# Searched per-batch orders, a rewritten first batch and a new load order in an attention-plus-MLP kernel

## The chip, the cores and the metric

One core of a Trainium2 chip. The metric is the device time of one launch in microseconds (us), which includes about 2 us outside the span of the profile. A run over 1.5% above the fastest of its kernel counts as slow. "PE" is TensorE, "DVE" VectorE, "ACT" ScalarE, "POOL" GpSimd.

## The reference

Eight batches of Nystrom attention (8 heads, 576 tokens, head size 64, 32 landmarks), then one MLP with squared ReLU over all 4608 tokens.

```python
q_lm, k_lm = segment means of q, k over 18 tokens each          # 32 landmarks
A  = softmax(q @ k_lm.T / 8);  Bm = softmax(q_lm @ k_lm.T / 8);  C = softmax(q_lm @ k.T / 8)
Z  = Bm.T / (norm1(Bm) * norminf(Bm) + 1e-6)
for _ in range(6): Z = 2*Z - Z @ Bm @ Z                          # iterative inverse
x   = A @ Z @ C @ v                                              # per head, then heads side by side
out = relu(x @ w_in)**2 @ w_out                                  # w_in 512x2048, w_out 2048x512
```

## The kernel before

It never forms x. For each batch it makes G = (Z C v) w_in, of which each half is 128 x 2048, and AT, the transposed A. A hidden block of 128 features, called h, is four matmuls of 288 columns from AT and G; then relu on ACT, the square on DVE, and 16 matmuls with w_out for each output tile. The six iterations of the inverse are three joint steps, a last joint step and two Newton steps, each with its products on PE and its update on DVE. In the steady state PE runs the h blocks of batch b, output tiles of earlier batches, and the small attention products of batch b+1 in between. The places of all of these are written as strings, which are followed token by token. PE, DVE and ACT work through their queues in that order.

```python
# tokens: h = one h block, s = its square, a number = so many output matmuls,
# mk mq = segment means, tk tq tt = transposes, lm ls = landmark scores and softmax, ib if = start of
# the inverse, jo jl = joint steps, nu nn = B times v and Newton step, sq sk tl = scores with exp,
# as ar at = A's row sums, rows, transposes, cv = C v, wt gg = fold and G, pk pq = cast of next k, q
BATCH0 = (
    "h h s s g h pk s h s h h g s h s h s tk0 h h s pq mk s h s h mq tq0 h s s 2 lm ls s h "
    "tk1 ib tq1 1 h h 1 tt 1 if 2 s 1 sq0 1 jo s 2 sq1 jo s 1 tl jo 2 as0 3 sk1 jl 3 ar0 3 "
    "sk0 2 as1 1 nu at0 2 ar1 nn pk+ 1 cv 1 nu nn1 1 at1 wt pq+ 2 gg0 2 gg1"
)
...                                                   # BATCH1, EVEN, ODD, LAST
PLANS = [BATCH0, BATCH1, EVEN, ODD, EVEN, ODD, EVEN, LAST]
```

The first batch has nothing beside which it could run. Its order is code, and PE's gaps are partly filled with warm-up matmuls, whose results nobody reads, to keep PE's clock up.

```python
def warm(n, width=512):
    z = bds[1].rearrange("p a b c -> p (a b c)")
    for _ in range(n):
        nc.tensor.matmul(idle[:, 0:width], lhsT=z[:, 0:P], rhs=z[:, 0:width], start=True, stop=True)
...
if first:
    prepare(0, ("k",))                # cast k: half on DVE, half on ACT
    load_rest(X["cast"])              # w_in(0), v0, w_in(1..3), q/k of batch 1, w_out x4, v1
    warm(3)
    k0 = transposed("k", 0)
    k1 = transposed("k", 1)
    kept = dve(*k0)
    ...                               # q's cast, means, landmark scores and softmax
    BT, ED = inverse_first(*begun)
    ...
for it in range(3):
    EY, ED, last = joint_step(EY, ED)
    ...                               # each step with a piece of A's or C's work aside
y, v = last_joint_step(EY, ED)
for it in range(2):
    UD = b_times_v(BT, v)
    y, v, last = newton_step(y, UD, it == 1)
    ...
wt, WT = folded_c(y.rearrange("p q a m -> p q (a m)"))
nc.scalar.copy(WT[:], wt[:])
warm(2)
...                                   # G from WT and w_in, copied by ACT and DVE; then h
```

The softmax here doesn't subtract the row's maximum and nothing guards it: scores larger than these inputs give would overflow.

## Time and profile before

| before | value | where it is read |
|---|---|---|
| time | 269.76 us (269.14 to 270.24) | three runs |
| span | 267.4 us | page |
| PE busy | 93% | page, part 1 |
| DVE, ACT busy | 66%, 59% | page, part 1 |
| first h block | 25.0 us | timeline of PE |
| first h block of batch 1 | 54.8 us | timeline of PE |

From the page of the kernel before: each digit is the busy share, in tenths, of one of 40 slices of 6.7 us, PEclk is the clock granted to PE.

```profile
PE   2988999699989999999999999999999999999994
DVE  4585989769983699559953798569943887443000
PEclk9997999999999999999999999999999999999999
```

PE is full but for the first 27 us and one slice near 50 us. The busy time by stretches (columns: stretch, its length, busy us and number of instructions of PE, PE's weight loads, DVE, ACT and POOL, then granted clock, DMA share, GB/s) says more:

```profile
20.00:25.00 5.00, 3.72 (x56) 1.79 (x53) 2.88 (x9) 2.41 (x7) 1.55 (x3) 0.70 1.40 197
25.00:37.00 12.00, 11.56 (x153) 8.58 (x147) 10.19 (x25) 10.79 (x23) 4.59 (x7) 0.98 1.32 204
37.00:54.00 17.00, 13.81 (x195) 7.72 (x196) 14.69 (x43) 9.26 (x15) 6.82 (x9) 1.00 1.53 198
```

In 20-25 us the granted clock is 0.70 on average: it is cut to half for part of the time. In 37-54 us PE is idle for 3.2 of 17 us. The timeline of PE (start, busy us, line, operation, count, and in brackets the idle time before and what ended it) has the landmarks of the head:

```profile
1.52 1.46 PE L234 MATMUL idle<-bd 128*128 128x512 bf16 x3 [1.52 <-DVE bd L90]
6.89 1.89 PE L258 MATMUL tps<-ident_bf,nat 128*128 128x128 bf16 x16 [3.90 <-POOL mask L142]
...
12.10 0.25 PE L315 MATMUL n<-STk,bd 128*128 128x32 bf16 x4
...
21.17 0.22 PE L357 MATMUL n<-y,U 32*32 32x32 bf16 x8 [0.39 <-ACT cvb L525]
...
24.99 1.33 PE L700 MATMUL h<-AT,G 128*128 128x288 bf16 x8
...
49.77 0.21 PE L357 MATMUL n<-y,ED 128*128 128x32 bf16 x2 [1.67 <-DVE ED L348]
```

The 16 transposes of k begin at 6.89 us, the landmark scores at 12.10, the last product of the inverse at 21.17, the first h at 24.99. One Newton step of batch 1 at 49.77 has made PE wait 1.67 us for DVE.

The pace of the first joint steps is in the timeline of DVE (L362 is the update, L464 a row sum of A):

```profile
15.81 0.29 DVE L362 SCALAR_TENSOR_TENSOR EY<-EY,n 128x128 bf16<-128x128 bf16 x1 [0.35 <-PE n L357]
16.01 0.41 DVE L464 TENSOR_REDUCE ra<-EA 128x8 f32<-128x256 f32 x1
16.45 0.29 DVE L362 SCALAR_TENSOR_TENSOR EY<-EY,n 128x128 bf16<-128x128 bf16 x1
```

### The profile page before, as it was taken

To read this page: it belongs to the slowest core of one execution; us is meant where nothing else is said; L and a number is where in the kernel's file an instruction comes from. 1 tells how busy PE (TensorE), PEld (TensorE's weight loads), DVE (VectorE), ACT (ScalarE), POOL (GpSimd) and SP (SyncE) were. 2 spreads that over 40 slices of the span, in tenths; PEclk is the share of its full clock that TensorE was granted. 3 is DMA by queue.
4 is the path that set the end of the run, shared out by engine and by line. 5 is a ranking of instruction groups with operands and counts; after the bars stand their busy time and mean duration, and the time that the engine had idled before them with its cause. 6 is when DMAs were issued, how large, how long until landed. Compare 5 with 4: busy or idle time off the path is not lost.

```text
span 267.4 us, 6750 instructions
## 1 busy us (share of the span) xinstructions
PE 247.7 (93%) x2752; PEld 151.0 (56%) x2793; DVE 177.4 (66%) x492; ACT 156.9 (59%) x278; POOL 45.5 (17%) x70
## 2 busy tenths in 40 slices
PE   2988999699989999999999999999999999999994
PEld 0754675276645665466546666466536665555443
DVE  4585989769983699559953798569943887443000
ACT  2366895377844774478345855487535955566210
POOL 8844233402400213021300122000000000000000
PEclk9997999999999999999999999999999999999999
DMA  8999999999699949995996579974421111111222
GB/s 184 177 204 196 204 205 189 206 210 165 103 161 214 126 95 158 142 206 99 201 159 132 78 94 171 168 134 110 90 81 40 42 39 42 39 43 39 78 81 78
DMA packets 69791, 34.65 MB, mean 130 GB/s; under 512 B 37376, under 2 KB 64256, under 8 KB 69760
## 3 DMA queue, kind: packets, MB, share of 16 engines
q0 software_dynamic: 39808, 17.83, 54.9%
q1 hardware_dynamic: 24704, 7.08, 17.7%
q10 hardware_dynamic: 5248, 9.31, 10.5%
q8 instruction: 22, 0.36, 0.6%
q14 instruction: 9, 0.07, 0.1%
HBM read 36.70 MB, written 9.44 MB: 173 GB/s over the span
## 4 chain that ended last, share of the span: by engine, by line
PE 60%; DVE 22%; DMA 6%; ACT 6%; issue 4%; POOL 2%; ACTq 0%; POOLq 0%; DVEq 0%
PE ops L732 18%; PE n L732 15%; PE h L700 14%; DMA raw<-in_q_dram 6%; DVE gT L708 5%; PE g L639 3%; DVE ra L464 3%; ACT r L707 3%; PE n L285 2%; DVE nat L220 2%; PE n L357 2%; PE n L486 2%; DVE ED L348 1%; DVE EY L362 1%; DVE rra L469 1%
## 5 line engine op out<-in xcount | busy, mean ns | idle before, releaser
L707 ACT ACTIVATE r<-h 128x576 bf16<-128x576 f32 x128 | 81.3, 655 | 40.6 <-PE h L700 30.1
L700 PE MATMUL h<-AT,G 128*128 128x288 bf16 x512 | 81.0, 286 | 0.7 <-ACT r L707 0.4
L732 PE MATMUL ops<-w_out_bf,gT 128*128 128x512 bf16 (+1 forms) x301 | 76.7, 368 | 1.0 <-issue 0.5
L708 DVE TENSOR_TENSOR gT<-r 128x576 bf16<-128x576 bf16 x128 | 55.5, 446 | 31.5 <-ACT r L707 30.7
L732 PEld LDWEIGHTS <-gT 128*128 128x128 bf16 x592 | 53.4, 97 | 40.6 <-issue 5.1
L732 PE MATMUL n<-w_out_bf,gT 128*128 128x512 bf16 x253 | 67.6, 379 | 0.9 <-issue 0.5
L700 PEld LDWEIGHTS <-G 128*128 128x128 bf16 x512 | 47.5, 98 | 22.3 <-issue 1.5
L628 DVE CAST G<-g 128x1024 bf16<-128x1024 f32 x14 | 17.1, 1224 | 10.5 <-PE g L639 10.5
L628 ACT CAST G<-g 128x1024 bf16<-128x1024 f32 x14 | 14.2, 1013 | 14.7 <-PE g L639 14.7
L743 ACT COPY o_sb<-ops 128x512 f32<-128x512 f32 (+1 forms) x19 | 10.9, 576 | 12.3 <-PE ops L732 11.9
L743 ACT COPY o_sb<-n 128x512 f32<-128x512 f32 x17 | 10.0, 585 | 10.9 <-PE n L732 10.3
L109 POOL DMA_DIRECT2D qkt<-in_k_dram x8 | 5.7, 708 | 54.3 <-PE n L295 42.7
L440 PEld LDWEIGHTS <-T 128*128 128x128 bf16 x256 | 11.2, 98 | 4.3 <-issue 1.0
L464 DVE TENSOR_REDUCE ra<-EA 128x20 f32<-128x640 f32 (+1 forms) x19 | 13.4, 705 | 0.3
L476 DVE TENSOR_TENSOR an<-EA,rra 128x640 bf16<-128x640 f32 (+2 forms) x17 | 13.1, 771 | 0.0
L440 PE MATMUL n<-bd,T 128*128 128x64 bf16 x256 | 12.7, 193 | 0.2
L357 PEld LDWEIGHTS <-ED 128*128 128x128 bf16 x84 | 7.1, 97 | 9.3 <-DVE ED L348 5.9
L121 POOL DMA_DIRECT2D raw<-in_k_dram x7 | 6.2, 884 | 32.4 <-DVE EY L362 12.4
L444 ACT ACTIVATE EA<-n 128x512 f32<-128x512 f32 x16 | 9.5, 595 | 2.3 <-PE n L440 2.3
L444 ACT ACTIVATE EC<-n 128x512 bf16<-128x512 f32 x16 | 9.6, 598 | 2.1 <-PE n L440 2.1
L220 DVE COPY nat<-raw 128x2048 bf16<-128x2048 bf16 x14 | 10.3, 734 | 0.6 <-DMA raw<-in_q_dram 0.4
L639 PE MATMUL g<-w_in_bf,WT 64*32 64x512 bf16 x232 | 9.6, 390 | 0.7 <-ACT G L628 0.4
(121 smaller groups left out, 268.1 us busy)
## 6 DMA issues: line engine op xcount, KB each, us to landing
out_dram<-o_sb ACTq DMA_DIRECT2D x31, 256.0 KB, 3.2
vm<-in_v_dram POOLq DMA_DIRECT2D x8, 512.0 KB, 16.4
raw<-in_k_dram POOLq DMA_DIRECT2D x7, 512.0 KB, 9.9
raw<-in_q_dram POOLq DMA_DIRECT2D x7, 512.0 KB, 13.8
w_in_bf<-in_moe_w_in_dram POOLq DMA_DIRECT2D x4, 512.0 KB, 10.7
w_out_bf<-in_moe_w_out_dram POOLq DMA_DIRECT2D x4, 512.0 KB, 16.1
out_dram<-o_sb ACTq DMA_DIRECT2D x9, 128.0 KB, 3.2
raw<-in_k_dram SPq DMA_DIRECT2D x1, 1024.0 KB, 5.3
```

The lines of the kernel that those rows point to most:

```text
L220: nc.vector.tensor_copy(X[nm][:], raw)
L440: nc.tensor.matmul(sc[:, c, j, :, :], lhsT=X[nm + "T"][:, c, p, :], rhs=BD[:, 1 if nm == "q" else 0, p, 0:64], start=True, stop=True)
L444: nc.scalar.activation((EA if nm == "q" else EC)[:, qd, 0:NC4, :], sc.rearrange("p c j i m -> p c (j i m)"), AF.Exp, scale=SCALE)
L464: nc.vector.reduce_sum(ra[:, quads, lo:hi, :], EA[:, quads, lo:hi, :].rearrange("p q c (h m) -> p q c h m", m=M), axis=AX.X)
L476: nc.vector.tensor_tensor(an[:, i, lo:hi, :].rearrange("p c (h m) -> p c h m", m=M), EA[:, i, lo:hi, :].rearrange("p c (h m) -> p c h m", ...
L628: last = (act, dve)[n % 2](G[:, :, n * 512:n * 512 + 512], gg[:])
L639: nc.tensor.matmul(g[i][M * p:M * p + M, :], lhsT=WT[64 * i:64 * i + 64, i, M * p:M * p + M], rhs=w_in_bf[64 * i:64 * i + 64, p, n * 512:n ...
L700: last = nc.tensor.matmul(h[:, j, 0:HALF], lhsT=G[:, qd, f * P:(f + 1) * P], rhs=AT[:, qd, j * HALF:(j + 1) * HALF], start=(qd == 0), stop ...
L707: nc.scalar.activation(r.rearrange("p (j t) -> p j t", j=2), h[:, :, 0:HALF], AF.Relu)
L708: return lambda: nc.vector.tensor_tensor(gT[:, f, o:o + S], r[:], r[:], ALU.mult)
L732: nc.tensor.matmul(ops, lhsT=gT[:, f, t * P:t * P + P], rhs=w_out_bf[:, f, i * n:i * n + n], start=(f == 0), stop=(f == NF - 1))
L743: nc.scalar.copy(o_h, ops)
```

## The change

Its intent: the orders of all eight batches come from a search (annealing) that rewards an early first h and few warm-up matmuls. The first batch becomes an order (HEAD) too. It takes four joint steps, the last one, and one B-times-v pair in place of three, one and two. G is made from C v alone while the inverse still runs, and Z is multiplied onto A instead ("az"). q and k of batches 0 to 2 are loaded to a staging area, and half of w_in goes behind q and k of batch 1. Batch 1 uses the compact inverse, with 32 x 32 tiles, that only batch 0 had. The two halves of k's and q's transposes have a PSUM tile each. The diff, cut to its core:

```diff
-PLANS = [BATCH0, BATCH1, EVEN, ODD, EVEN, ODD, EVEN, LAST]
+DMA_A = 9
+DMA_C = 9
+COMPACT = 1
+HEAD = (
+    "ck tk1 mk w:1:256 w:1:256 ek1d w:1:256 w:1 tk0 tt w:1 w:1 cq0 cq1 ek0a mq tq0 tq1 lm "
+    "w:1 et w:1:256 w:1 eq0a w:1:256 tl eq1d ls sum:0:4:5 w:1 ib w:1 w:1:256 sq1 w:1:256 if "
+    "sk1 sum:1:2:5 w:1:256 w:1 sum:1:0:2 jo w:1:256 w:1:256 rec:1 w:1:256 row:1:0:3 "
...
+    "jl at:0 ea0d ea1a ct w:1:256 nu w:1:256 g:0 gl1d fv w:1 gf1d w:1 gf0a az gl0d"
 )
+LOADS = "w10 v0 w00 q1 w01 w11 o0 o1 o2 o3 v1"
+PLANS = [
+    (
+        "pk h g:1 tt h pq h s tk1 s h s h tq1 s tk0 h h mk s s mq tq0 h lm s g:2 g:3 ls sk0 s h "
+        "h ib 1 h 1 s if tl h jo 1 sq0 s 1 jo s s 1 h jo 1 sq1 1 jl h 1 nu h s s h nn 2 sk1 nu s "
+        "1 s 8 as0 1 ar0 as1 2 ar1 5 nn1 cv 4 wt at0 2 gg0 2 at1 2 gg1 1"
+    ),
...                                                   # seven more
@@ load_rest
+        with tc.issue_after(behind[0].ins):
+            nc.gpsimd.tensor_copy(seg[:, NC4 + 2, :], seg[:, NC4, :])
+            for i in range(2):
+                ct = const.tile([P, 2, NC4 + 1, P], BF16, name="ct%d" % i)
+                nc.gpsimd.memset(ct[:], 0.0)
+                cts.append(ct)
@@ head_step
+            elif name == "az":
...
+                            nc.tensor.matmul(az[j][a:a + M, qd, 0:HALF],
+                                             lhsT=st["v"][a:a + M, qd, :],
+                                             rhs=AT[a:a + M, qd, j * HALF:j * HALF + HALF],
+                                             start=True, stop=True)
```

In HEAD, w:1 is one warm-up matmul 512 columns wide and w:1:256 one of 256; ck and cq cast k and q, ek and eq copy the transposes out, sum, rec and row are pieces of A's softmax, and a and d at the end of a token say ACT or DVE. The buffers ct belong to a variant for batches from DMA_C on; with DMA_C = 9 nothing reads them. HEAD has 35 warm-ups where there were 14.

## The prediction

> **What bounds it now.** TensorE. The page gives PE 247.7 us busy of 267.4 (93%), DVE 66%, ACT 59%. PE's 19.7 idle us are uneven. By windows, PE is busy 16.8 of the first 25 us, 13.8 of 17 us in 37-54, and 9.6 to 9.95 of every 10 us from 80 to 250. The timeline puts the first h matmul at 25.0 us, batch 1's first h at 54.8, and an even-odd pair of batches at 58.7 us. After the last matmul (263.8) come 3.6 us of copy and store. The h and output matmuls (128 groups of 0.49 us; 576 at 0.216) are about 187 us and stay.
>
> **What changes.**
>
> 1. Head. Before: three joint steps (0.63 us each), a last one, two Newton pairs (about 1.7 us each), then spread 0.29, fold matmul, copy 0.37, G matmul 0.63, G copy 0.37, with the transposed A landing late (ACT copy ending 25.2). Now: four joint steps, a last one, one pair; G is made from the C side meanwhile, and Z is multiplied onto A in small tiles. After the last DVE step (21.66 before) there remain one group of AZ matmuls and two 288-column copies, about 1.2 to 1.5 us, against 3.3. A joint step for a Newton pair is worth about 1 us more. DVE evacuations ahead of the landmark softmax give back a few tenths. First h: 21.7 us (20.8 to 23.2).
>
> 2. Clock. The granted clock is 0.70 in 20-25 and 0.98 in 25-37: about 3.4 us at half rate, after PE pauses at 20.4-22.7. The Trainium skill ("TensorE: Matmul & The Clock Gate", Part 1) gives one activity window as 3413 ns; this trace agrees. Warm-up matmuls rise from 14 to 35. I expect no half-clock stretch around the first h; its gain is inside item 1.
>
> 3. Batches 0 and 1. Before, batch 0's 16 h go in 25-38, paced by ACT (relu 0.65 us against 0.49 of matmul), then 37-54 has only 35 output matmuls to hide batch 1's inverse: 3.2 us idle, 1.8 of them one Newton step waiting for DVE. Now h is spread over the plan, batch 1 uses the compact inverse (no 0.29 us spreads), and 38 outputs fit: 4.5 us. First h of batch 1: about 47.5 us.
>
> 4. Loads. Same bytes, same 1024-column pieces; w_in's second half goes behind batch 1's q and k; q/k of batches 1 and 2 go to staging without a buffer wait. The DMA runs at about 200 GB/s through the first 50 us; batch 2's q lands at 51.75 before, by my estimate from bytes at 49.5 to 51 after. Its cast may hold DVE for 1 to 2 us, which caps item 3.
>
> 5. Steady state, 60-250: perhaps 2.5 us from reordering, mostly in 60-80. Tail unchanged.
>
> Sum: 3.3 + 4.5 + 2.5 = 10.3, less 0.8 for mis-modelled stalls: 9.5 us.
>
> **Prediction: 260.3 us, range 256.5 to 265.** Chances: faster by over 2% 0.88, within 2% 0.10, slower 0.02.
>
> **What would show it.** First h near 21.7; granted clock 1.00 in 20-30; PE idle in 37-54 about 1 us; batch 1's first h near 47.5, with DVE waiting for raw q near 50; pair period 58 us; 3.6 us after the last matmul.
>
> **What would make it wrong.** The head bound by the landing of q or w_in rather than the chain; warm-up matmuls standing ahead of chain steps on PE's ordered queue; DVE blocked at batch 1's early casts (k lands about 23 us by my estimate) so that squares and h buffers stall; the gain given back waiting for batch 2's loads; the searched orders losing over 2 us in the steady batches.

## The result

The changed kernel takes 265.97 us (265.86 to 266.55, 4 runs) against 269.47 (269.14 to 270.24, 4 runs). Ratios are computed as the mean time of one kernel's fast runs over that of the other's of the same rounds, so they are not quite the ratio of the medians quoted. The ratio is 0.987, with an interval of 0.984 to 0.990: 1.3% faster, which is within the 2% to which the prediction gave a chance of 0.10. Predicted was 260.3, in a range of 256.5 to 265. The measured time lies above the range.

The page after:

```profile
PE   0799899999999999999999999999999999999994
DVE  3488986879985779689766589689776884232100
PEclk9999999999999999999999999999999999999999
```

The stretches that answer to those of before:

```profile
20.00:25.00 5.00, 4.78 (x134) 3.07 (x134) 4.06 (x14) 1.86 (x5) 3.12 (x4) 1.00 1.46 201
25.00:37.00 12.00, 10.54 (x157) 7.16 (x146) 11.21 (x21) 10.05 (x19) 5.70 (x8) 1.00 1.20 208
37.00:54.00 17.00, 16.46 (x243) 9.43 (x245) 12.74 (x37) 9.98 (x20) 5.35 (x7) 1.00 1.51 200
```

The half clock in 20-25 is gone and 37-54 has only 0.5 us of idle PE, as predicted. But 25-37 has become worse, with 1.5 us idle. And the head is not earlier, by the timeline of PE:

```profile
8.01 1.03 PE L315 MATMUL tps<-ident_bf,nat 128*128 128x128 bf16 x8 [8.01 <-ACT nat L720]
...
9.41 1.23 PE L297 MATMUL idle<-bd 128*128 128x256 bf16 x4
10.44 1.06 PE L315 MATMUL tps<-ident_bf,nat 128*128 128x128 bf16 x8
...
11.72 1.06 PE L297 MATMUL idle<-bd 128*128 128x512 bf16 x2
...
14.29 0.26 PE L374 MATMUL n<-STk,bd 128*128 128x32 bf16 x4
...
23.77 0.22 PE L416 MATMUL n<-U,y 32*32 32x32 bf16 x8
...
25.68 0.65 PE L824 MATMUL h<-AZ,G 128*128 128x288 bf16 x4 [0.41 <-DVE AZ L797]
```

Nothing runs on PE before 8.01 us; the 8 transposes start 107 ns apart again; the landmark scores begin at 14.29 us, 2.2 us later than before, and the first h at 25.68, 0.7 later. The spans by step, each the difference of two starts in these two traces:

| step, us | before | after | gain |
|---|---|---|---|
| start to k's cast (its load has landed) | 6.13 | 6.91 | -0.78 |
| k's cast to landmark scores | 5.97 | 7.38 | -1.41 |
| landmark scores to end of the last iteration step on DVE | 9.56 | 10.26 | -0.70 |
| from there to the first h | 3.33 | 1.13 | +2.20 |
| first h to first h of batch 1 | 29.82 | 29.99 | -0.17 |
| first h of batch 1 to the end | 212.60 | 209.16 | +3.44 |
| span | 267.41 | 264.84 | +2.57 |

The orders issue 41 output matmuls before the first h of batch 1 instead of 37, so 0.86 us (4 x 0.216) of the gain in the last stretch was paid for in the stretch before it. The traces were taken of one run each; the timed medians differ by 3.5 us, and the row of k's landing is within the scatter (over the runs below it came at 6.3 to 7.0 us in the changed kernel and its variants, and at 6.79 in c1, a variant of the kernel before).

The joint steps stand further apart on DVE (L421 is the update now; reciprocals and rows of A come between two of them):

```profile
18.28 0.28 DVE L421 SCALAR_TENSOR_TENSOR EY<-EY,n 128x128 bf16<-128x128 bf16 x1
18.48 0.27 DVE L579 RECIPROCAL rra<-ra 128x20 f32<-128x20 f32 x1
18.78 0.89 DVE L586 TENSOR_TENSOR an<-EA,rra 128x384 bf16<-128x384 f32 x2
19.59 0.28 DVE L421 SCALAR_TENSOR_TENSOR EY<-EY,n 128x128 bf16<-128x128 bf16 x1
```

One more line stands out, in the timeline of DVE of the changed kernel, beside that of POOL below it:

```profile
26.21 0.68 DVE L283 COPY nat<-stage 128x2048 bf16<-128x2048 bf16 x1
...
27.80 2.54 DVE L283 COPY nat<-stage 128x2048 bf16<-128x2048 bf16 x1
```

```profile
27.36 0.22 POOL L261 COPY seg<-seg 128x32 bf16<-128x32 bf16 x1
27.50 2.28 POOL L264 MEMSET ct<- 128x1280 bf16 x2
```

The same cast of 128 x 2048 took 0.68 us at 26.21 and 2.54 at 27.80, while POOL cleared the ct buffers from 27.50 to 29.78. The cast ends 0.55 us after the clearing does. The Trainium skill ("SBUF — State Buffer", Who interferes with whom) says that GpSimd and a DVE instruction in a 2-port perf mode, which a copy from SBUF to SBUF can enter, exclude each other for a whole instruction. Here the cast was held through both clearing instructions. That made the first theory.

### The profile page after: what moved, and what is told of

Its sections match the earlier page's. It is cut to its first block, busy times and chain, and to the rows that moved or that the text cites. A ratio compares the mean times of both kernels' runs of the same rounds, so it can differ in the third digit from the quotient of the medians.

```text
span 264.8 us, 6918 instructions
## 1 busy us (share of the span) xinstructions
PE 248.2 (94%) x2835; PEld 153.7 (58%) x2878; DVE 176.4 (67%) x485; ACT 158.5 (60%) x278; POOL 47.8 (18%) x73
## 4 chain that ended last, share of the span: by engine, by line
PE 87%; DVE 5%; DMA 2%; issue 2%; ACT 2%; ACTq 0%
PE ops L853 24%; PE h L824 22%; PE n L853 21%; PE n L532 3%; PE g L807 3%; DMA stage<-in_k_dram 2%; PE idle L297 2%; PE n L416 2%; PE n L344 2%; PE n L598 2%; PE n L616 1%; DVE nat L283 1%; DVE gT L829 1%; PE tps L315 1%; PE n L631 1%
## 5 line engine op out<-in xcount | busy, mean ns | idle before, releaser
L829 DVE TENSOR_TENSOR gT<-r 128x576 bf16<-128x576 bf16 x128 | 54.9, 448 | 26.3 <-ACT r L828 26.1
L824 PE MATMUL h<-AT,G 128*128 128x288 bf16 x448 | 71.0, 286 | 0.2
L853 PE MATMUL n<-w_out_bf,gT 128*128 128x512 bf16 x252 | 69.7, 379 | 1.1 <-issue 0.3
L864 ACT COPY o_sb<-ops 128x512 f32<-128x512 f32 (+1 forms) x19 | 10.9, 574 | 14.5 <-PE ops L853 14.5
L134 POOL DMA_DIRECT2D raw<-in_k_dram x5 | 4.6, 921 | 53.2 <-DVE gT L829 28.1
L574 DVE TENSOR_REDUCE ra<-EA 128x20 f32<-128x640 f32 (+3 forms) x19 | 13.2, 704 | 0.3 <-ACT EA L562 0.3
L532 PE MATMUL n<-bd,T 128*128 128x64 bf16 x256 | 12.7, 193 | 0.3 <-issue 0.2
L315 PEld LDWEIGHTS <-nat 128*128 128x128 bf16 x96 | 6.8, 108 | 9.8 <-ACT nat L720 8.0
L134 POOL DMA_DIRECT2D raw<-in_q_dram x5 | 4.4, 884 | 38.5 <-DVE rc L447 28.1
L315 PE MATMUL tps<-ident_bf,nat 128*128 128x128 bf16 x32 | 3.4, 278 | 8.0 <-ACT nat L720 8.0
L824 PE MATMUL h<-AZ,G 128*128 128x288 bf16 x64 | 10.0, 286 | 0.6 <-DVE AZ L797 0.4
```

The lines of the kernel that those rows point to most:

```text
L134: d = queue.dma_start(dst, src)
L315: nc.tensor.transpose(tps[:, i, p, :], X[nm][:, 2 * half + i, 2 * p:2 * p + 2, :].rearrange("p h d -> p (h d)"), ident_bf[:],)
L532: nc.tensor.matmul(sc[:, c, j, :, :], lhsT=X[nm + "T"][:, c, p, :], rhs=BD[:, 1 if nm == "q" else 0, p, 0:64], start=True, stop=True)
L574: nc.vector.reduce_sum(ra[:, quads, lo:hi, :], EA[:, quads, lo:hi, :].rearrange("p q c (h m) -> p q c h m", m=M), axis=AX.X)
L824: nc.tensor.matmul(h[:, j, 0:HALF], lhsT=G[:, qd, f * P:(f + 1) * P], rhs=AT[:, qd, a0 + j * HALF:a0 + (j + 1) * HALF], start=(qd == 0), s ...
L829: return lambda: nc.vector.tensor_tensor(gT[:, f, o:o + S], r[:], r[:], ALU.mult)
```

## The experiments

Fifteen kernels ran; all gave the right result. To compare heads, the table at the end of this section counts from k's cast, to take the chance of its landing out. Runs told together below ran on the same chip beside the same runs of before.

### First call: the head's start and the clearing

The theories: (a) PE is the chain of the head's start, because it is at half clock there and has six warm-ups ahead of q's means in its ordered queue; (b) the clearing of ct blocks DVE. The rival to both is that waiting for data sets these times.

**a0_same**: no edit.

> The changed kernel again, as the base of this call. All theories: 266.0 us, ratio to before 0.987, first h matmul at 25.3 to 25.8 us. If raw k lands near 6.1 us here instead of 6.9, the late landing in the first profile was chance and the first h comes about 0.6 us earlier.

Measured: 265.71 us, ratio 0.984; k's cast at 6.32, first h at 24.23. Landing and the clock's phase move the head by over a microsecond from run to run; the times of the six runs go from 264.5 to 266.4.

**a1_no_ct**

```diff
-                nc.gpsimd.memset(ct[:], 0.0)
```

> The two memsets of the ct buffers on GpSimd, which nothing reads, are taken out. Port theory (the DVE cast of batch 1's q stood 2.54 us instead of 0.68[...]): the cast takes 0.7 us, h matmuls of batch 0 come 1.5 to 1.9 us earlier after it, total 264.3 to 265.0 us. Rival (the cast was waiting for its data to land, the memsets are harmless): the cast starts later or stays long, total 266.0 us, same as the base.

Measured: 265.12 us, ratio 0.982. The timeline of DVE:

```profile
25.55 0.68 DVE L282 COPY nat<-stage 128x2048 bf16<-128x2048 bf16 x1
...
27.14 0.68 DVE L282 COPY nat<-stage 128x2048 bf16<-128x2048 bf16 x1
```

Both casts take 0.68 us, and the first h to batch 1's first h takes 29.00 us instead of 30.12. In the time it is worth 0.6 us by the medians, less than was expected and within the scatter of the base; in the trace the effect is plain.

**a2_early_warm**

```diff
-    "ck tk1 mk w:1:256 ...
+    "ck w:14 tk1 mk w:1:256 ...
```

> 14 warm-up matmuls at the very start, in time in which PE otherwise waits for k (0 to 8 us). Clock theory (the head is late because all PE work from 8.0 to 13.7 us runs at half clock and PE is the chain there): transposes of k issue every 56 ns instead of 104, the q means come 1.2 to 2 us earlier, first h near 24.0 us, total 264.2 to 265.0. Rival (the head is bound by q's landing and by the chain on DVE and ACT, not by PE): q means move by less than 0.5 us and the total stays within 0.4 us of the base.

Measured: 264.12 us, ratio 0.978. The timeline of PE:

```profile
1.53 5.67 PE L297 MATMUL idle<-bd 128*128 128x512 bf16 x14 [1.53 <-DVE bd L117]
7.82 0.62 PE L315 MATMUL tps<-ident_bf,nat 128*128 128x128 bf16 x8 [0.63 <-ACT nat L720]
...
12.08 0.26 PE L374 MATMUL n<-STk,bd 128*128 128x32 bf16 x4
```

The transposes issue every 56 ns; the trace's clock record has full speed from 6.6 us on. From k's cast to the landmark scores it is 5.36 us instead of 6.53: theory (a). In this run the clearing happened to miss the cast (0.69 us), so some of the gain is that luck.

**a3_no_late_warm**

```diff
-    "ck tk1 mk w:1:256 w:1:256 ek1d w:1:256 w:1 tk0 tt w:1 w:1 cq0 cq1 ek0a mq ...
+    "ck tk1 mk ek1d tk0 tt cq0 cq1 ek0a mq ...
```

> The six warm-up matmuls that stand in PE's ordered queue ahead of the q means (1.9 us at half clock) are taken out, nothing else. Queue theory (they delay the chain): q means start about 11.4 us, when q's cast is done, instead of 12.6; first h 0.8 to 1.2 us earlier; total 264.8 to 265.2. Rival (they only fill waiting time and buy the clock): the clock comes up a window (3.4 us) later, the first h does not move or comes later, total 266.0 to 267.

Measured: 264.15 us median (263.9 to 265.7), ratio 0.980. From k's cast to the scores it is 6.24 us, although the clock came up 6.0 us after the cast (4.6 in the base). The warm-ups there do stand ahead of the chain. The ratio's interval overlaps the base's, so the size in time stays rough.

### Second call: old orders, and the three repairs together

**b2_old01** and **b3_old27**: the old orders in the new kernel, for batches 0 and 1, and for batches 2 to 7.

```diff
-PLANS = [new0, new1, new2, ..., new7]
+PLANS = ["g:1 " + BATCH0 with its g as g:2, g:3, BATCH1 less 15 outputs, new2, ..., new7]   # b2
+PLANS = [new0, new1 plus 15 outputs, EVEN, ODD, EVEN, ODD, EVEN, LAST]                      # b3
```

> The changed kernel with the orders of batches 0 and 1 from before (15 output steps at the end of batch 1's order cut so that the same 84 outputs are issued by then). Theory one (the new order of batch 0 did take away about 3 us of waits of PE in the inverse of batch 1, and gave most of it back as more PE work and the stall of DVE): the old order is slower by 1 to 3 us, 267 to 268.5. Rival (the new orders of batches 0 and 1 are worth nothing): 265.7, as the base of the first call.

Measured: 275.62 us, ratio 1.022, far outside both expectations. The waits between 24 and 60 us (who waited for what, us in total, times, longest):

```profile
PE g L776 <- DMA w_in_bf<-in_moe_w_in_dram: 3.5, 2, 2.1
ACT G L614 <- PE g L776: 4.2, 2, 3.9
```

The old order asks for the third and fourth pieces of G early, and the new load order lands that half of w_in late. The test mixed two things, so b4 below repeats it.

> The changed kernel with the orders of batches 2 to 7 from before (EVEN, ODD and LAST; 15 output steps added to batch 1's order so that they start from the same count as before). Theory (the steady stages gained 2.6 us through the new orders, as the traces have it from batch 1's first h to the end): 267.8 to 268.8. Rival (that gain comes from the loads and from batch 1, not from these orders): 265.5 to 266.3.

Measured: 268.34 us, ratio 0.995. The theory holds: the new orders of batches 2 to 7 are worth 2.6 us against the base's 265.7.

**d1_combo**, **d2_combo_tk0**: early warm-ups in, the six taken out, nothing but DMA issues on POOL; in d2 also the half of k first that DVE casts.

```diff
-    "ck tk1 mk w:1:256 w:1:256 ek1d w:1:256 w:1 tk0 tt w:1 w:1 cq0 cq1 ek0a mq ...
+    "ck w:14 tk1 mk ek1d tk0 tt cq0 cq1 ek0a mq ...          # d1
+    "ck w:13 tk0 mk ek0d tk1 tt cq0 cq1 ek1a mq ...          # d2
-            nc.gpsimd.tensor_copy(seg[:, NC4 + 2, :], seg[:, NC4, :])
+    nc.vector.tensor_copy(seg[:, NC4 + 2, :], seg[:, NC4, :])      # early, after seg is made
-                nc.gpsimd.memset(ct[:], 0.0)
```

> 14 early warm-ups, none of the six ahead of the q means, no ct memsets, and the small seg copy moved from GpSimd to DVE early, so GpSimd has only DMA issues at 26 us. If the three effects are separate and add up: first h about 16.6 us after k's cast starts (17.0 with early warm-ups alone), DVE cast of batch 1's q 0.7 us, total 262.6 to 263.4. Rival (they share one critical stretch, so taking one away exposes another): no better than early warm-ups alone, 264.1.

Measured: 263.79 us, ratio 0.978. That is no better by ratio than early warm-ups alone. Early warm-ups and the removal of the six do not add up: they share the stretch up to the landmark scores (5.35 us after the cast against 5.36). On the clearing this comparison says little, because in a2's trace the cast had missed it (the stretch after the first h is 29.34 us in both).

> As the combination before, and the transposes begin with the half of k that DVE casts in 0.69 us rather than the half that ACT casts in 1.05 us. If the start of PE is what counts: PE begins 0.35 us earlier and the first h comes 0.2 to 0.35 us earlier than in the combination, total 262.3 to 263.1. Rival (q's casts on DVE are then the limit, at 11 us): first h within 0.1 us of the combination.

Measured: 263.51 us, ratio 0.977. The cast to the scores is 5.16 us and PE now waits 0.77 and 0.29 us for the two casts of q on DVE, of which the second waits 0.28 us for its load. The limit has moved to q's casts, in part to q's landing. From the cast to the first h it is 16.80 us against 16.79 in d1: the rival is right, the little start did not reach h.

### Third call

**b1_compact0**

```diff
-COMPACT = 1
+COMPACT = 0
```

> The changed kernel with the compact inverse for batch 0 alone, so batch 1's products are one 128-wide matmul pair on spread operands again. The prediction's theory (the compact form shortens batch 1's chain by the spreads of 0.29 us and helps): slower by 0.5 to 1.5 us, 266.2 to 267.2. Rival from the count of PE time (this stretch is full of PE work and the eight small products and the fp32 row sums cost PE 0.38 and 0.39 us more, while DVE has time to spare): the same or up to 0.5 us faster, 265.2 to 265.8.

Measured: 267.73 us, ratio 0.992. The compact inverse of batch 1 is worth 1.5 to 2.0 us (against e1, 266.28 us, and a0), at the top of what the prediction's own theory had it or above. My rival, built on counting PE time, is wrong: PE saves 1.2 us on the products and the row sums (0.65 against 1.42 + 0.39), but from first h to first h it is idle for 2.83 us against 1.18 in a0, with 1.08 and 0.36 us of it ahead of two of the inverse's products.

**b4_old01_loads**: b2 with the old load order.

```diff
-LOADS = "w10 v0 w00 q1 w01 w11 o0 o1 o2 o3 v1"
+LOADS = "w00 v0 w10 w01 w11 q1 o0 o1 o2 o3 v1"
```

> As the old orders of batches 0 and 1 that gave 275.6 us, with the loads in the order of before as well (both w_in halves ahead of batch 1's q and k). Theory (the 10 us came from G pieces 2 and 3 waiting for w_in's second half, which the new load order lands 6 us later): back to 266 to 268.5 us. Rival (the old orders do not fit the new head at all): stays above 272.

Measured: 271.57 us, ratio 1.007. It lies between the two: 4.0 us of the 9.9 were the loads. The remaining 5.9 us against the base belong to the old orders of batches 0 and 1 and the old loads together, in the new kernel; the trace has 3.3 of them between the two first h, and why was not followed further.

**c1_before_early_warm**: the kernel before with the early warm-ups.

```diff
-            warm(3)
+            warm(12)
             k0 = transposed("k", 0)
```

> The kernel before with 12 warm-up matmuls at the start instead of 3. If the half clock at the start costs the same in both kernels, it is no part of the change's effect: k's transposes at 56 ns, first h 1 to 1.8 us earlier after k's cast than the 18.9 us of before, total 268.0 to 268.8 against 269.8. Rival (only the new head has PE in the chain there): within 0.4 us of before.

Measured: 269.72 us, ratio 0.999. The cast to the scores fell from 5.97 to 5.01 us, but the first h came only 0.4 us earlier after the cast. The busy time by stretches shows where the rest went:

```profile
20.00:25.00 5.00, 4.25 (x73) 2.23 (x65) 2.77 (x9) 2.18 (x7) 1.49 (x2) 0.55 1.35 197
25.00:37.00 12.00, 11.66 (x138) 7.94 (x131) 9.33 (x21) 10.45 (x21) 4.64 (x6) 0.90 1.34 203
37.00:54.00 17.00, 15.43 (x195) 8.35 (x193) 14.87 (x47) 9.52 (x16) 7.52 (x9) 0.92 1.53 199
```

Half-clock stretches follow, of 6.8 us from 20.5 and of 3.4 us from 51.2 by the trace's records. My reading is that the old head has too few matmuls later on to keep the clock that the early ones bought; no run added any there, but f2 below tests the same in the new head.

**e1_seg_moved**: the clearing kept, only the small copy moved off POOL.

```diff
-            nc.gpsimd.tensor_copy(seg[:, NC4 + 2, :], seg[:, NC4, :])
+    nc.vector.tensor_copy(seg[:, NC4 + 2, :], seg[:, NC4, :])      # early, after seg is made
```

> The changed kernel with the memsets kept, but the small seg copy taken off GpSimd (done early on DVE). In two profiles the long DVE cast (2.65 and 2.78 us) overlapped that copy on GpSimd, which itself stood 2.41 us instead of 0.22, and the memsets came after by the record. If the copy alone locks with the cast: the cast is 0.7 us, total 264.8 to 265.3. If the memsets do it: the cast is still long (2 to 2.6 us) where it starts inside them, total 265.5 to 265.9.

Measured: 266.28 us, ratio 0.987, no gain. DVE, then POOL:

```profile
27.04 3.06 DVE L283 COPY nat<-stage 128x2048 bf16<-128x2048 bf16 x1
```

```profile
27.26 2.29 POOL L264 MEMSET ct<- 128x1280 bf16 x2
```

The cast took 3.06 us with the clearing inside it, so the clearing blocks it without the copy, and the cast again ends 0.55 us after the clearing. The cast's record begins 0.22 us ahead of the clearing's, so the one whose record begins first was not the one that went first.

### Fourth call: what was still open

**f1_ls_first** (on d2):

```diff
-... w:1:256 tl eq1d ls sum:0:4:5 ...
+... w:1:256 tl ls eq1d sum:0:4:5 ...
```

> The best combination so far (263.5 us), with DVE's landmark softmax ahead of its copy of q's second half, as in the kernel before. If DVE's ordered queue paces the head: landmark scores to first h 11.0 to 11.2 us instead of 11.6, total 263.0 to 263.3. Rival (the copy must be done anyway before the scores and the work only changes places): 11.5 to 11.7 us, total 263.5 or a little more.

Measured: 263.50 us, ratio 0.978; scores to first h 11.79 us against 11.64 in d2. The rival is right: moving one copy does not shorten the head.

**f2_no_mid_warm** (on d2): all 29 warm-ups after the landmark scores removed.

```diff
-    "... lm w:1 et w:1:256 w:1 eq0a w:1:256 tl ..."
+    "... lm et eq0a tl ..."                                 # and so on to the end of HEAD
```

> The best combination with all 29 warm-ups after the landmark scores taken out, the 13 at the start kept. If they keep the clock: one or two half-clock stretches of 3.4 us between 15 and 30 us, first h 0.3 to 1 us later and batch 0's h stretched, total 264.3 to 266. If they only stand in PE's queue: no such stretch, first h the same or up to 0.5 us earlier, total 263.0 to 263.6.

Measured: 265.09 us, ratio 0.984, so 1.6 us slower than d2.

```profile
12.00:20.00 8.00, 5.32 (x143) 3.88 (x143) 7.18 (x28) 4.62 (x10) 3.94 (x7) 0.87 1.46 192
20.00:25.00 5.00, 3.96 (x57) 1.72 (x55) 3.58 (x9) 2.00 (x7) 2.83 (x4) 0.50 1.43 201
25.00:37.00 12.00, 11.71 (x153) 8.77 (x146) 9.10 (x24) 10.56 (x19) 4.05 (x6) 0.87 1.20 208
```

PE stands at half clock for 10.2 us (17.9 to 28.1 by the clock records). The many warm-ups of the change are part of its gain. The run also settles something else: with no warm-up left in PE's queue there, the first three joint steps on DVE lie 1.31 and 0.85 us apart (1.31 and 0.91 in the changed kernel), and PE waits for DVE before the third step's product:

```profile
16.90 0.24 PE L410 MATMUL n<-EY 32*32 32x64 bf16 x8 [1.08 <-DVE EY L415]
```

So what stands between these steps on DVE sets their pace, not the warm-ups on PE.

**b5_new_old_loads**: new orders, old load order (the edit of b4 alone).

> The changed kernel with its new orders and the load order of before (both w_in halves ahead of batch 1's q and k). If the new orders need the new loads: DVE stands at the casts of batch 1's k and q, which then land some 5 us later by the bytes ahead of them, h matmuls of batch 0 stand behind it, total 268 to 271. If the load order is worth little with these orders: 265.7 to 266.5.

Measured: 271.69 us, ratio 1.009, so 6.0 us slower than the base. DVE, whose work before had ended at 24.6 us:

```profile
28.42 2.26 DVE L283 COPY nat<-stage 128x2048 bf16<-128x2048 bf16 x1 [3.85 <-DMA stage<-in_k_dram]
```

It waited 3.85 us for k of batch 1 to land, and the cast then met the clearing. The new orders of batches 0 and 1 and the new loads belong together: undoing the orders alone costs 9.9 us (b2), the loads alone 6.0, both 5.9 (b4).

### The heads side by side

All in us, from one trace each; "clock full" is when the trace's records first have PE's clock at full speed.

| run | k's cast starts | clock full | cast to scores | scores to first h | first h to batch 1's first h | time |
|---|---|---|---|---|---|---|
| before | 6.13 | 11.7 | 5.97 | 12.89 | 29.82 | 269.5 |
| the change | 6.91 | 13.7 | 7.38 | 11.39 | 29.99 | 266.0 |
| a0_same | 6.32 | 10.9 | 6.53 | 11.38 | 30.12 | 265.7 |
| a1_no_ct | 6.60 | 12.2 | 7.03 | 11.39 | 29.00 | 265.1 |
| a2_early_warm | 6.72 | 6.6 | 5.36 | 11.67 | 29.34 | 264.1 |
| a3_no_late_warm | 6.76 | 12.7 | 6.24 | 11.39 | 30.24 | 264.2 |
| b1_compact0 | 6.39 | 13.0 | 7.29 | 11.39 | 31.29 | 267.7 |
| c1_before_early_warm | 6.79 | 6.8 | 5.01 | 13.48 | 30.58 | 269.7 |
| d1_combo | 6.88 | 6.6 | 5.35 | 11.44 | 29.34 | 263.8 |
| d2_combo_tk0 | 6.37 | 4.8 | 5.16 | 11.64 | 29.32 | 263.5 |
| f1_ls_first | 6.44 | 6.3 | 5.03 | 11.79 | 29.01 | 263.5 |
| f2_no_mid_warm | 6.50 | 4.2 | 5.04 | 12.14 | 30.62 | 265.1 |

The nine traces whose head is the change's (the change, a0, a1, b1 to b5, e1) show where its scatter comes from. The time from the cast to the scores follows the time from the cast to the full clock: 6.19 us at 3.85 (b5), 6.53 at 4.58 (a0), 7.03 at 5.61 (a1), 7.38 at 6.80 (the change). From the scores to the first h all nine take 11.4 us, or 11.7 in b2 and b4, which make one more piece of G first. By my estimate from these numbers a3, with its clock full after 5.99 us, would have needed about 7.1 us with its six warm-ups, against 6.24.

d2_combo_tk0 and f1_ls_first are the best versions found, about 2.3 us under the changed kernel's 265.7 to 266.0 and 6 us under the kernel before.

## Why the prediction was right or wrong

**Item 1, the head: wrong.** The step "First h: 21.7 us" failed; it was 25.68 (23.96 to 25.68 over the nine traces with this head), against 25.0 before. From k's cast it is 17.6 to 18.9 us against 18.9 in the one trace of before, so at most 1.3 us were gained where 3.3 were forecast. Three terms make that up.

- *The end of the head was right.* From the last iteration step to the first h: predicted 1.2 to 1.5 us against 3.3, measured 1.13 against 3.33.
- *"A joint step for a Newton pair is worth about 1 us more" failed.* I priced a joint step at the 0.63 us it had before. In the new order the starts of the steps on DVE lie 1.31, 0.91, 1.03 and 0.98 us apart (18.28, 19.59, 20.50, 21.53, 22.51), and sums and rows of A stand between them on DVE. From the first joint step to the end of the last Newton step it takes 6.27 us (18.28 to 24.55), against 5.85 before (15.81 to 21.66): 0.42 lost where about 1 was to be gained. The other 0.28 us of the 0.70 lie ahead of the first step, about the "few tenths" that the prediction did allow. From the scores to the last step DVE is busy 8.59 of 10.26 us; before it was 7.39 of 9.56. The count of steps is the same, six, and the cheaper kind was to save time, while the work in DVE's ordered queue between the steps rose. From 17.14 to 22.3 us DVE has no idle time above 0.04 us, so each of the four joint steps began when DVE's instruction before it ended, and f2 shows that the warm-ups on PE do not set this pace. f1 shows that moving one copy does not help; no run took work off DVE, so what that would gain is not measured.
- *The start was not in the sum at all.* From k's cast to the landmark scores the change lost 0.2 to 1.4 us (6.19 to 7.38 over the nine traces, against 5.97). PE runs at half clock there, has no early warm-up, begins with the half of k that ACT casts in 1.05 us, and works through six warm-ups ahead of q's means. a2 and a3 show the clock and the warm-ups; starting with DVE's half brought nothing at the first h (d2). The prediction named "warm-up matmuls standing ahead of chain steps" as what could make it wrong, and then gave it no time; and it says nothing of the clock there, which the page's 9s show as full and transposes 107 ns apart as half.

**Item 2, the clock: right.** No half-clock stretch stands near the first h in the changed kernel; f2 shows that the added warm-ups in the middle of the head do this, and that it is worth about 1.6 us there; c1 fits. The timed runs of the kernel before say what the half clock cost it: of its 37 fast runs, the 8 with a mean granted clock of 0.997 or more took 269.0 us on average, the 4 with 0.981 took 271.6, and all of them 269.8, while the changed kernel's own runs have 0.999 or more. By that estimate a clock that stays up is about 0.8 us of the whole gain.

**Item 3, batches 0 and 1: wrong.** "4.5 us" and "first h of batch 1: about 47.5 us" failed: the stretch from one first h to the next went from 29.82 to 29.99 us, where the sum wanted 25.8. Most of the waits did go. Counting on PE the time from each matmul's start to the next one's, by kind, and PE's idle time in a row of its own:

| first h to batch 1's first h, us | before | the change | a1_no_ct |
|---|---|---|---|
| PE idle | 3.69 | 1.75 | 0.36 |
| h blocks, with waits | 9.04 | 10.05 | 8.92 |
| output matmuls, with waits (37, 41, 41 in the orders) | 8.88 | 8.55 | 9.76 |
| inverse and fp32 row sums, with waits | 2.71 | 2.26 | 1.81 |

The first two traces lack the records of five output matmuls each (32 of 37 and 36 of 41 are there), so some of their time is booked on other kinds or as idle; a1 has all 41. In a1 28.6 of the 29.0 us are PE work; before, 26.1 of 29.8 were. The prediction took PE's waits as gain and did not ask how much work the new orders put in their place: four more output matmuls (0.86 us, given back later), a piece of G that before was made ahead of the first h, row sums on PE, and eight products in place of two. On top, the clearing on POOL stopped DVE and through it the h blocks by 1.1 us (30.12 to 29.00, a0 to a1), a term that the diff shows in plain sight and that I did not cost. The compact inverse was right in sign, at 1.5 to 2.0 us (b1).

**Item 4, the loads: the cap named was not the one that mattered.** In the changed kernel DVE did not wait for q of batch 2. But "same bytes" hid that order is worth 6 us (b5).

**Item 5, the steady stages: right in size.** 2.5 us predicted; 3.44 less 0.86, so 2.6, in the traces for batches 1 to 7, and 2.6 by b3 for batches 2 to 7 alone. "Mostly in 60-80" fits less well: there PE's idle time fell from 1.05 to 0.21 us in the two traces, while b3, with the old orders from batch 2 on, is idle for 1.6 us between 80 and 100 us where a0 has none.

Together: the sum was 3.3 + 4.5 + 2.5 less 0.8. The traces gave -0.7, -0.2 + 0.9 and +2.6, so 2.6 us. In the timed runs it is 3.5 to 4.0 us; the profiled run was the slowest of its four (266.55 us), with k landing late and the clock late.

## What to carry to other kernels

When a wait is taken off the busiest engine, count the work that moves in its place before calling the wait a gain; and price a step of a chain by what will stand ahead of it in its engine's ordered queue, not by what it took in the old order. Read the clock from the spacing of equal matmuls as well as from the clock row. In a diff, cost every instruction, also those on an engine that is 18% busy and whose result nobody reads.

## What the Trainium skill lacked or had wrong

- No page has it: the profile's granted clock reads full before the trace's first clock record, although equal transposes start 107 ns apart until then and 56 ns apart after it.
- "TensorE: Matmul & The Clock Gate" (Part 1) does say that the window is free-running, so that the point of transition varies, by 500 ns to either side; here, with pauses in PE's work, full clock came 2.8 to 5.7 us after PE's first matmul (10.2 to 13.7 us after the start) over the nine profiled runs whose head is the change's.
- "TensorE: Matmul & The Clock Gate" (Part 1) calls the warm-up a budget of some 3.4 us. Early warm-ups alone bought nothing in the old kernel (c1: 269.72 against 269.75 us, fast runs), and its trace has the clock falling back for 6.8 us at 20.5. In the 3.4 us ahead of that fall PE's longest single pause was 0.5 us (0.6 us ahead of the fall at 22.0 in the kernel before), so no long pause came before either.
- "SBUF — State Buffer" (Who interferes with whom) says that whoever issues first takes the shared ports. In e1 the DVE cast's record begins at 27.04 us and the clearing's at 27.26, yet the cast ended at 30.1, after the clearing (29.5). In a0, a3, b1 and b3 the cast and the small GpSimd copy both stood about 2.4 to 2.8 us, and by the record the clearing came only after them; no run here shows what resolved it, and records on GpSimd are rough.
